# A tiled FFT-domain convolution: frequency ranges of the first tiles, the last tile's scratch in parts, and inverse work behind the last round

## The chip, the cores and the metric

The kernel runs on one core of a Trainium2 chip. The metric is the device time of one execution in microseconds (us). Eight runs of the kernel before gave a median of 279.88 us (278.17 to 282.5). All other numbers come from one further execution that the hardware profiler recorded.

The core has five engines that run their own instruction streams and wait for each other by semaphores: TensorE (PE in the profile; PEld is its weight load), VectorE (DVE), ScalarE (ACT), GpSimd (POOL) and SyncE (SP), which here only issues DMAs. TensorE writes its products into eight PSUM banks; VectorE and ScalarE copy ("evacuate") them to SBUF.

## The reference

```
x: (1, 224, 224, 96) bf16    w: (7, 7, 96, 96) bf16
wp = pad(w, H and W up to 224)
Yf = einsum('bhwi,hwio->bhwo', rfft2(x), rfft2(wp))
y  = irfft2(Yf, (224, 224)).astype(bf16)
```

This is a circular convolution of a 224 x 224 image of 96 channels with a 7 x 7 kernel, 96 channels in and 96 out.

## The kernel before

The kernel transforms only along the height, by small DFT matrices, and convolves along the width directly. The height is cut into 8 blocks of B = 28 rows; each needs L = 34 input rows, which give NS = 17 frequencies with a real and an imaginary part. The width is cut into NT = 7 tiles of 32 columns, numbered 0 to 6 in the code; the text counts them first to seventh, and the seventh (TL = 6) is the last one. Even and odd columns are kept apart as two phases.

Each tile passes three stages:

- *Forward.* TensorE multiplies the pixels of one column (118 rows, four of the eight blocks at a time) with the DFT matrix `Fm`; the result goes through PSUM into `xf`, by channel, frequency, column and block. For the tiles from the fourth on, `a_jobs` makes all 17 frequencies of a column with one matmul of 136 columns. For the first three tiles `f_jobs(t, part)` does it by frequency ranges, so that the rounds of the first frequencies can begin early; the limits are in `SH2`. A tile's `xf` begins with three columns (the halo) that `new_xf` copies on ScalarE from the tile before, one copy per phase and range. The buffers `xf` alternate between tiles.
- *Rounds.* `b_round(t, s, ...)` handles one frequency s: 33 matmuls of 96 columns, with the input planes as stationary operand (from `xf` and from `J`, sums and differences of planes that `jit` makes on VectorE, three frequencies as one group) and the transformed filters `WF` as moving operand. ScalarE copies a part of the products to `tt_`, VectorE makes `u` and `v`, and the sum of `v` and `u` goes to `yf` on GpSimd or, in some rounds (`ydve`), on VectorE. After a group of frequencies (`YGRP`) the `yf` tile is written to a scratch tensor in DRAM (`scr`).
- *Inverse.* The scratch is read back with frequency and block in the partitions (`tt`), and `c_jobs(t)` makes 11 jobs of two matmuls each with the inverse DFT matrix `G`; each job's two products are copied out and written to the result. Loads for these jobs are issued by `queue_c` in round 3 of the next tile (all are issued by SP) as far as buffers are free.

The rounds of the first two tiles are interleaved with lag `LAG` = 4; r counts these steps. From the third tile on, tiles follow one another. Everything else (filter transform in the first two tiles, forward of the next tile, inverse jobs of the two tiles before) is put between the matmuls of the rounds as filler. A queue entry `add(a, b, jobs)` spreads its jobs evenly over the slots a to b; a round s has slots 2s (`mid`) and 2s + 1 (`end`). How many inverse jobs run in each tile is in `CQ`: (jobs left from two tiles before, jobs of the tile before). In the loop over tiles, `km` is the slot where the old ones end and the new ones begin, and `k1` the slot where all must be done.

Which engine evacuates a PSUM bank is decided by `evac` when the program is built, from running estimates `load["v"]` and `load["a"]`.

The last tile has no rounds after it to hide its inverse. Its scratch has separate tensors: `scra` for frequencies 0 to 8 and `scrb` 0 and 1 for 9 to 14 and 15 to 16. `scra` is loaded in round 11. At the end `load_b` loads the other two; the inverse is then done with all blocks at once: `first` multiplies with `GA` (frequencies 0 to 8), `WARM` matmuls on zeros keep TensorE running, and `second` adds the product with `GB`. The copies alternate between VectorE and ScalarE (`tail_evac`). `GA` and `GB` are put together from `G` by 20 small DMAs (`g_parts`), one per round in the fourth and fifth tiles.

The writes of the last tile's `yf` are put in a list `puts` and issued from ScalarE's queue in the round after, but for the last one, which SP issues.

Of the kernel before, what the change touches and what calls it, by code (L numbers as in the profile page):

```python
# [8 lines left out]
BF16 = mybir.dt.bfloat16  # L9
# [5 lines left out]
B = 28  # L15
# [28 lines left out]
WARM = 36  # L44
BIAS = 3000.0


# [5 lines left out]
def kernel(  # L53
# [76 lines left out]
    def dma(out_ap, in_ap):  # L130
        return DE.dma_start(out=out_ap, in_=in_ap)
# [9 lines left out]
    KB = (NJ * 2 * (SB - SA), NJ * 2 * (NS - SB))  # L141
    assert sum(KB) == 128
    XW = 2 * TW * C
    xn_bufs = [cpool.tile([R, XW + 32], BF16, name=f"xn{i}") for i in range(2)]

# [320 lines left out]
    def b_round(t, s, mid, end, ydve=False, planes=()):  # L466
# [26 lines left out]
        if s == 0:  # L493
            for part in range(2):
                conv(b0, part * C, 0, part)
            SE.copy(out=tt_[:, 0:2 * C], in_=b0[:, 0:2 * C])
            mid()
            for mi, m in enumerate((2, 1)):
                for part in range(2):
                    conv(b1, (mi * 2 + part) * C, m, part)  # L500
            VE.tensor_tensor(out=yv.rearrange("p r m o -> p m r o"),
                             in0=tt_[:, 0:2 * C].rearrange("p (r o) -> p r o", o=C).unsqueeze(1).to_broadcast([128, 2, 2, C]),
                             in1=b1[:, 0:4 * C].rearrange("p (m r o) -> p m r o", m=2, r=2), op=ALU.add)
            load["a"] += 110 + 0.9 * 192
            load["v"] += 540
            for f in planes:
                f()
            end()
        else:
            v = tv_pool.tile([128, 2, 2, C], F32, name="v")  # L510
            if merge:
                conv(b0, 2 * C, 0, 0, both=True)
                conv(b0, 2 * C, 2, 0, add=True)
                conv(b0, 3 * C, 1, 0, add=True)
                conv(b0, 0, 0, 1)
                conv(b0, C, 0, 2)
# [37 lines left out]
        if s == y1 - 1:  # L554
            dst, yo0 = scr_tiles[t], 0
            if t == TL:
                i = (s >= SA) + (s >= SB)
                dst, yo0 = scr_tiles[(t, i)], (0, SA, SB)[i]

            def put(eng=DE):  # L560
                eng.dma_start(out=dst.rearrange("w j s e -> (w j) s e")[:, y0 - yo0:y1 - yo0],
                              in_=yf[:, 0:y1 - y0].rearrange("p s r m o -> p s (r m o)"))
            if t == TL and s < NS - 1:
                puts.append(lambda: put(SE))
            else:
                put()
# [20 lines left out]
    tl_a = [tl_all[0:KA, g * TW2:(g + 1) * TW2].rearrange("p (w e) -> p w e", e=2 * C) for g in range(2)]  # L587
    tl_b = tl_all[:, 2 * TW2:3 * TW2].rearrange("p (w e) -> p w e", e=2 * C)

    def load_b(i, eng, nh):  # L590
        sb = scr_tiles[(TL, 1 + i)].rearrange("w j s (r e) -> (j s r) w e", r=2)
        for h in range(nh):
            w0, w1 = h * TW // nh, (h + 1) * TW // nh
            eng.dma_start(out=tl_b[i * KB[0]:i * KB[0] + KB[i], w0:w1], in_=sb[:, w0:w1])

    def g_parts():
        for j in range(4):
            dma(GA[j * 2 * SA:(j + 1) * 2 * SA, j * B:(j + 1) * B], G[0:2 * SA, 0:B])
            yield
        for j in range(NJ):  # L600
            for i, (s, s1) in enumerate(((SA, SB), (SB, NS))):
                n = 2 * (s1 - s)
                dma(GB[i * KB[0] + j * n:i * KB[0] + (j + 1) * n, j // 4, j % 4 * B:(j % 4 + 1) * B], G[2 * s:2 * s1, 0:B])
                yield

    yo_free = [J_bufs[2][0:4 * B, i * PXC * C:(i + 1) * PXC * C] for i in range(2)]
# [63 lines left out]
    for jg in range(2):  # L670
        for f in a_bank(0, xf0, xh_bufs[jg], 0, 3, jg, 0):
            f()
    fj = [f_jobs(0, p) for p in range(3)]
    for p in range(3):
        for f in fj[p][0]:
            f()
    for _ in range(3):
# [48 lines left out]
    nburst = len(bursts)  # L726
    for r in range(NS + LAG):
        if r == 0:
            add(0, 4, fj[1][1] + fj[2][1])
        for p in range(3):  # L730
            if r == (1, 3, 5)[p]:
                new_xf(1, SH2[p], SH2[p + 1])
                fj = f_jobs(1, p)
                if p == 2:
# [3 lines left out]
        for p in range(3):  # L738
            if r == SH2[p + 1] + 1 - (p == 2):
                new_xf(2, SH2[p], SH2[p + 1])  # L740
                fj = f_jobs(2, p)
                if p == 2:
# [32 lines left out]
    for t in range(2, NT):  # L775
        if t == TL:
            scr_tiles[t] = None
            scr_tiles[(t, 0)] = dr_pool.tile([TW, NJ, SA, 4 * C], BF16, name="scra")
            for i in range(2):
                scr_tiles[(t, 1 + i)] = dr_pool.tile([TW, NJ, (SB - SA, NS - SB)[i], 4 * C], BF16, name=f"scrb{i}")  # L780
# [17 lines left out]
        for s in range(NS):  # L798
# [3 lines left out]
                now = jit(t, g + 1) if g + 1 < len(JGB) else jit(t + 1, 0)  # L802
            if s == 3:
                queue_c(t - 1)
            if t in (3, 4):
                next(gp, None)
            if t == TL and s == SA + 2:
                sv = scr_tiles[(TL, 0)].rearrange("w j s (r e) -> (j s r) w e", r=2)
                for g in range(2):
                    for p0, p1 in ((0, 64), (64, KA)):  # L810
                        dma(tl_a[g][p0:p1], sv[g * KA + p0:g * KA + p1])
            b_round(t, s, fills(qs, 2 * s), fills(qs, 2 * s + 1), bool(now) or (t == TL and s >= NS - 3), now)
    tail[0] = 2
    assert not cj and not pend
# [22 lines left out]
    for i, (g, q) in enumerate(order):  # L837
# [41 lines left out]
```

## Time and profile before

| | us |
|---|---|
| median of 8 runs | 279.88 |
| the profiled execution | 280.32 |
| its span in the trace | 278.6 |
| first round begins | 22.3 |
| fourth to sixth tiles and most of the third | about 100 to 227 |
| last tile's rounds begin on TensorE | 227.1 |
| last sum `yf` ends | 261.0 |
| first product with `GB` | 268.56 |
| last copy ends | 272.9 |

The page shows for each engine the busy time and its share of the span. Its second part cuts the span into 40 slices of 7 us and gives each engine's busy share in tenths; PEclk is the clock that TensorE was granted, in tenths.

```profile
PE   8979998999999999999999999999999997999791
```

The costliest groups, with the mean ns of one instruction, are these; the matmul's duration includes its latency, so that starts lie closer together than durations:

```profile
L85 PE MATMUL pb<-WF,J 96*128 96x96 bf16 x2898 | 168.3, 206 | 0.8 <-DVE WF L85 0.3
...
L85 POOL TENSOR_TENSOR yf<-v,u 128x384 bf16<-128x384 f32 x85 | 84.6, 1011 | 150.1 <-issue 96.4
...
L85 ACT CAST xf<-pb 96x408 bf16<-96x408 f32 (+2 forms) x147 | 68.8, 486 | 6.4 <-PE pb L85 4.3
...
L85 DVE TENSOR_TENSOR J<-xf 96x1824 bf16<-96x1824 bf16 (+1 forms) x84 | 60.0, 753 | 0.1
...
L85 PE MATMUL pb<-Fm,xn 118*128 118x136 bf16 (+3 forms) x640 | 45.7, 199 | 0.4 <-DVE u L85 0.4
...
L85 PE MATMUL pb<-tt,Gm 102*84 102x384 bf16 (+1 forms) x132 | 33.0, 331 | 2.3 <-DMA tt<-scr 2.3
```

All are on line 85, because a helper issues every instruction; the names of the tiles tell what they are. The last column is the engine's idle time just before such an instruction, and what ended most of it.

### The profile page before, as it was taken

Reading aid. Unit: us, or ns where it says so; the run is one execution under the profiler, and the core shown is the slowest. Engines: PE = TensorE matmul, PEld = TensorE weight load, DVE = VectorE, ACT = ScalarE, POOL = GpSimd, SP = SyncE. Lnnn points to the kernel's source line nnn. Section 1 sums busy time; section 2 is a strip of 40 time slices with the busy share of each in tenths; the row PEclk is TensorE's granted clock in tenths of the full one; section 3 lists DMA queues with packets and bytes.
Section 4 is the critical chain, followed back from the end, with each engine's and each line's share of the span. In section 5 each row is a group of like instructions: output and inputs, shape, how many; then the busy total and the mean of one; then the engine's idle time right before and its main releaser. Section 6 shows DMA issues by size and latency. Waiting matters only on the chain. (4 is left out here: it accounts for less than half of the span.)

```text
span 278.6 us, 12291 instructions
## 1 busy us (share of the span) xinstructions
PE 263.8 (95%) x5226; PEld 242.3 (87%) x5226; DVE 218.8 (79%) x457; ACT 198.9 (71%) x489; POOL 98.0 (35%) x146
## 2 busy tenths in 40 slices
PE   8979998999999999999999999999999997999791
PEld 3659898999999999999999999999999996889670
DVE  5538899898799798779887888779788899488432
ACT  5539996677964767988988799887989855475122
POOL 7720032443545745323422423341532242223000
PEclk9999999999999999999999999999999999799997
DMA  7957010722111497798975496989498428755955
GB/s 185 214 108 200 16 47 2 232 68 87 45 47 46 146 260 133 228 282 225 285 204 180 115 292 166 274 192 336 155 208 249 144 94 212 194 157 166 236 121 164
DMA packets 46038, 46.79 MB, mean 168 GB/s; under 512 B 35150, under 2 KB 36954, under 8 KB 45886
## 3 DMA queue, kind: packets, MB, share of 16 engines
q1 hardware_dynamic: 43696, 43.94, 57.7%
q10 hardware_dynamic: 2288, 2.06, 2.6%
q8 instruction: 41, 0.67, 1.1%
q14 instruction: 13, 0.11, 0.1%
HBM read 24.65 MB, written 21.33 MB: 165 GB/s over the span
## 5 line engine op out<-in xcount | busy, mean ns | idle before, releaser
L85 PE MATMUL pb<-WF,J 96*128 96x96 bf16 x2898 | 168.3, 206 | 0.8 <-DVE WF L85 0.3
L85 PEld LDWEIGHTS <-J 96*128 96x128 bf16 x2898 | 142.8, 98 | 10.7 <-issue 1.6
L85 POOL TENSOR_TENSOR yf<-v,u 128x384 bf16<-128x384 f32 x85 | 84.6, 1011 | 150.1 <-issue 96.4
L85 ACT CAST xf<-pb 96x408 bf16<-96x408 f32 (+2 forms) x147 | 68.8, 486 | 6.4 <-PE pb L85 4.3
L85 PE MATMUL pb<-WF,xf 96*128 96x96 bf16 x952 | 60.6, 207 | 1.2 <-DVE WF L85 0.6
L85 DVE TENSOR_TENSOR J<-xf 96x1824 bf16<-96x1824 bf16 (+1 forms) x84 | 60.0, 753 | 0.1
L85 PEld LDWEIGHTS <-xf 96*128 96x128 bf16 x952 | 47.4, 98 | 1.6 <-issue 1.0
L85 PE MATMUL pb<-Fm,xn 118*128 118x136 bf16 (+3 forms) x640 | 45.7, 199 | 0.4 <-DVE u L85 0.4
L85 PE MATMUL pb<-tt,Gm 102*84 102x384 bf16 (+1 forms) x132 | 33.0, 331 | 2.3 <-DMA tt<-scr 2.3
L85 ACT CAST WF<-pb 96x480 bf16<-96x480 f32 (+1 forms) x58 | 28.6, 572 | 7.3 <-PE pb L85 7.3
L85 ACT CAST J<-pb 84x384 bf16<-84x384 f32 (+1 forms) x66 | 28.3, 483 | 6.1 <-PE pb L85 3.1
L85 ACT CAST yo<-pb 84x384 bf16<-84x384 f32 (+1 forms) x66 | 28.1, 483 | 4.7 <-PE pb L85 4.7
L85 PEld LDWEIGHTS <-xn 118*128 118x128 bf16 x640 | 30.5, 97 | 0.5 <-issue 0.5
L85 DVE TENSOR_TENSOR J<-J 96x912 bf16<-96x912 bf16 (+1 forms) x42 | 25.0, 595 | 0.0
L85 PE MATMUL pb<-wq 98*128 98x120 bf16 (+1 forms) x288 | 21.3, 226 | 1.4 <-DMA wq<-in_w_dram 1.4
L85 PEld LDWEIGHTS <-wq 98*128 98x128 bf16 x288 | 19.4, 150 | 1.9 <-issue 1.9
L85 PE MATMUL pb<-wu 128*128 128x512 bf16 (+1 forms) x80 | 17.8, 385 | 1.0 <-DVE ct L85 1.0
L85 PEld LDWEIGHTS <-wu 128*128 128x128 bf16 (+1 forms) x80 | 9.3, 118 | 8.5 <-issue 2.7
L85 DVE TENSOR_TENSOR yf<-v,u 128x384 bf16<-128x384 f32 x27 | 15.5, 574 | 0.9
L85 DVE CAST WF<-pb 96x480 bf16<-96x480 f32 (+1 forms) x14 | 8.1, 612 | 7.6 <-PE pb L85 7.5
L85 PEld LDWEIGHTS <-Gm 102*84 102x84 bf16 (+1 forms) x132 | 11.1, 118 | 3.0 <-DMA tt<-scr 2.4
L85 ACT COPY xf<-xf 96x816 bf16<-96x816 bf16 (+3 forms) x20 | 11.1, 616 | 0.0
(391 smaller groups left out, 228.8 us busy)
## 6 DMA issues: line engine op xcount, KB each, us to landing
scr<-yf SPq DMA_DIRECT2D x30, 288.0 KB
xn<-in_x_dram SPq DMA_DIRECT2D x12, 672.0 KB
tt<-scr SPq DMA_DIRECT2D x24, 336.0 KB
out_dram<-yo SPq DMA_DIRECT2D x12, 252.0 KB
out_dram<-J SPq DMA_DIRECT2D x12, 252.0 KB
tt<-scr SPq DMA_DIRECT2D x6, 288.0 KB
wq<-in_w_dram SPq DMA_DIRECT2D x1, 1719.0 KB
WF<-in_x_dram SPq DMA_DIRECT2D x2, 672.0 KB
```

The costliest lines, as they stand in the source:

```text
L85: r = fn(*a, **k)
```

## The change

- `SH2` has two ranges, 0 to 7 and 8 to 16, instead of three; `f_jobs` of the first three tiles is called for two parts. The second range has 72 columns per matmul (9 frequencies, two parts, four blocks). In the second tile the ranges start in steps r = 1 and 3 (before 1, 3, 5), in the third in r = 9 and 17 (before 9, 14, 17).
- The last tile's scratch has six tensors of three frequencies (the last of two), `PARTS`. `load_p(i)` loads one of them: parts 0 to 3 in rounds 6, 9, 12 and 15, parts 4 and 5 after the last round, all issued by SP. The order of rows in `GA` and `GB` follows, so `g_parts` issues 36 DMAs, now in the fourth to sixth tiles.
- The last part's write is issued by ScalarE.
- `CQ`: of the inverse jobs, the fifth tile's rounds run 13 instead of 14, the sixth tile's 12 instead of 14, the last tile's 10 instead of 14. The seven that are left, all of the sixth tile, stand behind the last round, before `first`. In the last tile the old jobs fill slots 3 to 15 and the new ones follow until slot 26.
- `WARM` is 20 instead of 36.
- The result of the last tile is written in eight DMAs of 8 columns instead of four of 16.
- One estimate for VectorE's load in the first two tiles is 350 instead of 250.

```diff
-SB = 15
+PARTS = (0, 3, 6, 9, 12, 15, 17)
...
-CQ = {2: (11, 0), 3: (11, 2), 4: (9, 5), 5: (6, 8), 6: (3, 11)}
-SH2 = (0, 8, 13, 17)
+CQ = {2: (11, 0), 3: (11, 2), 4: (9, 4), 5: (7, 5), 6: (6, 4)}
+SH2 = (0, 8, 17)
...
-WARM = 36
+WARM = 20
...
+    prt = []
+    for a, b in zip(PARTS[:-1], PARTS[1:]):
+        prt.append((a, b, int(a >= SA), (4 if a < SA else NJ) * 2 * (a - (0 if a < SA else SA))))
...
-            load["v"] += (560 if ydve else 250 if t < 2 else 0) + (560 if merge else 900)
+            load["v"] += (560 if ydve else 350 if t < 2 else 0) + (560 if merge else 900)
...
-                i = (s >= SA) + (s >= SB)
-                dst, yo0 = scr_tiles[(t, i)], (0, SA, SB)[i]
+                i = sum(s >= b for b in PARTS[1:])
+                dst, yo0 = scr_tiles[(t, i)], PARTS[i]
...
-            if t == TL and s < NS - 1:
+            if t == TL and s == NS - 1:
+                put(SE)
+            elif t == TL:
                 puts.append(lambda: put(SE))
...
-    def load_b(i, eng, nh):
...
+    def load_p(i):
+        a, b, h, r0 = prt[i]
+        sv = scr_tiles[(TL, i)].rearrange("w j s (r e) -> (j s r) w e", r=2)
+        n = 2 * (b - a)
+        if h:
+            dma(tl_b[r0:r0 + NJ * n], sv)
+        else:
+            for g in range(2):
+                dma(tl_a[g][r0:r0 + 4 * n], sv[g * 4 * n:(g + 1) * 4 * n])
...
     def g_parts():
...
+        for a, b, h, r0 in prt:
+            n = 2 * (b - a)
+            for j in range(NJ if h else 4):
...
-            if r == (1, 3, 5)[p]:
+            if r == (1, 3)[p]:
...
-                add(2 * r + 1, 2 * r + (5, 5, 4)[p], fj[0] + fj[1])
+                add(2 * r + 1, 2 * r + (5, 8)[p], fj[0] + fj[1])
...
-            if r == SH2[p + 1] + 1 - (p == 2):
+            if r == (9, 17)[p]:
...
-                add(2 * r, 2 * r + (8, 7, 5)[p], fj[0] + fj[1])
+                add(2 * r, 2 * r + (10, 6)[p], fj[0] + fj[1])
...
-        k1 = 2 * NS if t < TL else 2 * NS - 6
+        k1 = 2 * NS if t < TL else 2 * NS - 8
...
+        if t == TL:
+            km = 15
...
-            if t in (3, 4):
+            if t in (3, 4, 5):
                 next(gp, None)
-            if t == TL and s == SA + 2:
...
+            if t == TL:
+                for i, (_, b, _, _) in enumerate(prt[:4]):
+                    if s == b + 3:
+                        load_p(i)
...
-    load_b(0, SE, 2)
-    load_b(1, DE, 1)
+    load_p(4)
+    load_p(5)
+    for f in cj:
+        f()
...
-        if q % 4 == 3:
-            w0 = TL * 2 * TW + q // 4 * PXC
-            dma(out[0, g * M4:(g + 1) * M4, w0:w0 + PXC, :].rearrange("h w c -> h (w c)"), yo[0:M4])
+        if q % 2:
+            w0, o0 = TL * 2 * TW + (q - 1) * 4, (q - 1) % 4 * 4 * C
+            dma(out[0, g * M4:(g + 1) * M4, w0:w0 + 8, :].rearrange("h w c -> h (w c)"), yo[0:M4, o0:o0 + 8 * C])
```

More of the change, by code (lines that the diff above doesn't have):

```diff
@@ L140 @@
     KA = 4 * 2 * SA
-    KB = (NJ * 2 * (SB - SA), NJ * 2 * (NS - SB))
-    assert sum(KB) == 128
+    prt = []
+    for a, b in zip(PARTS[:-1], PARTS[1:]):
+        prt.append((a, b, int(a >= SA), (4 if a < SA else NJ) * 2 * (a - (0 if a < SA else SA))))
+    assert SA in PARTS and NJ * 2 * (NS - SA) == 128
     XW = 2 * TW * C
@@ L588 @@
     tl_b = tl_all[:, 2 * TW2:3 * TW2].rearrange("p (w e) -> p w e", e=2 * C)
-    def load_b(i, eng, nh):
[L591 to L594, printed above, removed]
-    def g_parts():
[L597 to L603, printed above, removed]
+    def load_p(i):
[7 more added lines that the diff above has]
+                dma(tl_a[g][r0:r0 + 4 * n], sv[g * 4 * n:(g + 1) * 4 * n])
+    def g_parts():
+        for a, b, h, r0 in prt:
+            n = 2 * (b - a)
+            for j in range(NJ if h else 4):
+                o = GB[r0 + j * n:r0 + (j + 1) * n, j // 4] if h else GA[r0 + j * n:r0 + (j + 1) * n]
+                dma(o[:, j % 4 * B:(j % 4 + 1) * B], G[2 * a:2 * b, 0:B])
                 yield
@@ L672 @@
             f()
-    fj = [f_jobs(0, p) for p in range(3)]
-    for p in range(3):
+    fj = [f_jobs(0, p) for p in range(2)]
+    for p in range(2):
         for f in fj[p][0]:
@@ L728 @@
         if r == 0:
-            add(0, 4, fj[1][1] + fj[2][1])
-        for p in range(3):
-            if r == (1, 3, 5)[p]:
+            add(0, 4, fj[1][1])
+        for p in range(2):
+            if r == (1, 3)[p]:
                 new_xf(1, SH2[p], SH2[p + 1])
                 fj = f_jobs(1, p)
-                if p == 2:
+                if p == 1:
                     for jg in range(2):
                         fj[jg][-1] = then_load(fj[jg][-1], 2, jg)
-                add(2 * r + 1, 2 * r + (5, 5, 4)[p], fj[0] + fj[1])
-        for p in range(3):
-            if r == SH2[p + 1] + 1 - (p == 2):
+                add(2 * r + 1, 2 * r + (5, 8)[p], fj[0] + fj[1])
+        for p in range(2):
+            if r == (9, 17)[p]:
                 new_xf(2, SH2[p], SH2[p + 1])
                 fj = f_jobs(2, p)
-                if p == 2:
+                if p == 1:
                     for jg in range(2):
                         fj[jg][-1] = then_load(fj[jg][-1], 3, jg)
-                add(2 * r, 2 * r + (8, 7, 5)[p], fj[0] + fj[1])
+                add(2 * r, 2 * r + (10, 6)[p], fj[0] + fj[1])
         if r == PGRP[-2][1] + 1:
@@ L777 @@
             scr_tiles[t] = None
-            scr_tiles[(t, 0)] = dr_pool.tile([TW, NJ, SA, 4 * C], BF16, name="scra")
-            for i in range(2):
-                scr_tiles[(t, 1 + i)] = dr_pool.tile([TW, NJ, (SB - SA, NS - SB)[i], 4 * C], BF16, name=f"scrb{i}")
+            for i, (a, b, _, _) in enumerate(prt):
+                scr_tiles[(t, i)] = dr_pool.tile([TW, NJ, b - a, 4 * C], BF16, name=f"scrl{i}")
         else:
@@ L804 @@
                 queue_c(t - 1)
-            if t in (3, 4):
+            if t in (3, 4, 5):
                 next(gp, None)
-            if t == TL and s == SA + 2:
[L808 to L811, printed above, removed]
+            if t == TL:
+                for i, (_, b, _, _) in enumerate(prt[:4]):
+                    if s == b + 3:
+                        load_p(i)
             b_round(t, s, fills(qs, 2 * s), fills(qs, 2 * s + 1), bool(now) or (t == TL and s >= NS - 3), now)
     tail[0] = 2
-    assert not cj and not pend
-    load_b(0, SE, 2)
-    load_b(1, DE, 1)
+    assert not pend
+    load_p(4)
+    load_p(5)
+    for f in cj:
+        f()
     if NP2:
```

## The prediction

> **What bounds the kernel now.** I read the page first, then busy time by stretches, then the order of time where a stretch looked wrong, then the chain.
>
> ```profile
> PE 263.8 (95%) x5226; PEld 242.3 (87%) x5226; DVE 218.8 (79%) x457; ACT 198.9 (71%) x489; POOL 98.0 (35%) x146
> ...
> PEclk9999999999999999999999999999999999799997
> ```
>
> TensorE is the bound almost everywhere, at full clock but for slice 35 (index 34) and the last. The stretches:
>
> ```profile
> core 0: us, PE busy (x) PEld busy (x) DVE busy (x) ACT busy (x) POOL busy (x), PEclk, DMA share, GB/s
> ...
> 36.00:50.00 14.00, 13.27 (x334) 13.08 (x333) 13.74 (x26) 11.16 (x30) 4.37 (x5) 1.00 0.11 41
> ...
> 99.80:228.10 128.30, 127.90 (x2563) 119.84 (x2560) 107.74 (x227) 107.81 (x276) 44.48 (x45) 1.00 0.77 214
> 228.17:234.75 6.58, 6.58 (x139) 6.15 (x136) 6.11 (x13) 2.94 (x8) 3.48 (x4) 1.00 0.51 136
> 234.75:241.00 6.25, 3.99 (x45) 3.44 (x44) 3.04 (x8) 3.17 (x8) 0.99 (x1) 0.73 0.85 190
> ...
> 228.17:261.00 32.83, 29.77 (x561) 27.07 (x558) 26.76 (x56) 17.31 (x44) 10.37 (x11) 0.95 0.70 176
> ```
>
> From 99.8 to 228.1 TensorE has no gap. From 36 to 50 VectorE is as full (13.74 of 14) and TensorE idles 0.73. From 234.75 to 241 something is wrong: 3.99 busy of 6.25 at clock 0.73. In order of time:
>
> ```profile
> 231.67 7.50 SPq L85 DMA_DIRECT2D tt<-scr  x7
> ...
> 237.06 0.72 PE L85 MATMUL pb<-tt,Gm 102*84 102x384 bf16 x2 [2.26 <-DMA tt<-scr]
> ...
> 237.90 0.84 PE L85 MATMUL pb<-WF,xf 96*128 96x96 bf16 x8
> ```
>
> The first inverse job of the sixth tile waits for its load, and afterwards TensorE runs slow: eight matmuls take 0.84 where they otherwise show 0.50. The end:
>
> ```profile
> 261.03 0.35 SPq L85 DMA_DIRECT2D scrb<-yf  x1
> ...
> 262.35 5.82 PEld L85 LDWEIGHTS <-wu 128*112 128x112 bf16 x36
> ...
> 264.31 0.33 SPq L85 DMA_DIRECT2D xf<-scrb  x1
> ...
> 268.56 0.97 PE L85 MATMUL pb<-xf,GB 128*112 128x384 bf16 x5
> ...
> 270.01 3.77 SPq L85 DMA_DIRECT2D out_dram<-tt  x4
> ```
>
> The last sum ends at 261.0; its round trip through DRAM and the 36 filler matmuls both last until about 268.5, so 7.56 us hold no useful TensorE work except four first products. Then come 4.4 us of copies and a write that lands 3.3 us after its issue (the waits of SP's queue).
>
> **What the Trainium skill says.** "TensorE: Matmul & The Clock Gate", Back-to-back issue gap: small matmuls have a floor of about 25 ns, wider ones take N/2.4 + 2.5 ns. The trace agrees: 24 of 40 columns run from 91.77 to the next start at 92.37 (25 ns each), 16 of 32 columns in 0.41 (26), 8 of 64 in 0.23 (29), 6 of 136 in 0.36 (60). Same page, What's actually happening: an idle TensorE falls to half clock by windows of 3.4 us, which run free. Here 2.26 us idle dropped it, and 1.64 us idle (260.2 to 261.84) did not. "DMA: Bandwidth & Descriptors", Two DMAs through the same engine are not ordered: a reader must wait for the writer's semaphore; here the load of the last part issues 3.3 us after its write does. Same page, Issuing engines are not separate DMA queues: so putting the last write on ScalarE's queue buys no bandwidth, as far as this trace can say.
>
> **The change, part by part.** Gains are in us of the profiled execution (280.32, span 278.6, so 1.7 around it; the median, 279.88, is 0.44 lower).
>
> 1. *Forward in two ranges.* Per tile, 64 positions (two halves of rows, 16 columns, two phases) had three matmuls, 29 + 26 + 26 = 81 ns, and now have two: 29 and one of 72 columns, which the trace lacks; the bounds are 29 (the 64-column row) and 60 (136 columns), the page's formula gives 32.5, an estimate that I take. The saving is 19 ns x 64 = 1.2 per tile (at 60 ns it would be a loss of 0.5). Half of the first tile's lies before the weights arrive at 17.8 and is hidden. Left are 2.5 x 1.2 = 3.1 of TensorE time. Evacuations stay 20 per tile with the same elements; two halo copies go in each of the second and third tile (ScalarE, about 0.3 each). The new estimate of 350 for VectorE moves little: in the instruction order, copies of the weights and the forward on VectorE go from 19 to 19. So VectorE keeps its 13.74 of 36 to 50, where most of the second tile's last two ranges sit: I credit 0.3 of its 1.2. Of the first tile's 0.6, with ScalarE at 12.78 of 13.7 there, 0.3. For the third tile the second range is now one block in rounds 17 to 20, with 12 copies on ScalarE instead of 4: 12 x 0.45 + 4 x 0.31 + 1.2 of halo = 7.8 against TensorE's 4 x 1.40 + 64 x 0.0325 = 7.7, balanced; the rounds 14 to 16 before it lose their filler and then run at 1.40 each on TensorE, against about 1.48 on VectorE (u and v together 0.81, a J group of 2.0 per three rounds). I credit 0.7 of 1.2. Sum 1.3; from 0 (VectorE sets it all) to 3.1.
>
> 2. *Jobs moved out of the fifth and sixth tiles' rounds.* The job counts per tile go from 14 and 14 to 13 and 12. A job's two matmuls hold TensorE 0.33 (229.44 to 229.77). 3 x 0.33 = 1.0 in the stretch without a gap; ScalarE, at 84%, loses work too. Full credit: 1.0.
>
> 3. *The last tile's rounds.* Before, tile 5's first job is due at slot 9, 3 us after its load could issue (231.67, when the scratch had landed). Now six old jobs fill slots 3 to 15 and the first new one comes at slot 15, three rounds (over 4.2 us) later, while the data took until 237.06, 2.26 beyond slot 9. The stall of 2.26 goes, and so does the slow clock after it: 237.06 to 240.94 took 3.88 where the same sequence takes 2.24 at full clock, so 1.64. Four fewer jobs: 1.3. TensorE alone: 5.2. What is late next is VectorE: it has 26.76 busy in 32.83, and 32.83 - 5.2 = 27.6 would ask 97% of it. It reached 98% in 36 to 50, but with TensorE idling 5%. I take 28.6, a gain of 4.2; between 3.3 (29.5, VectorE at 91%) and 5.2.
>
> 4. *Six parts.* Same bytes. Loads of parts 0 to 3 are issued in rounds 6, 9, 12 and 15, three rounds after their writes (about 4.8 us; a write of 288 KB took 4.83 with its issue in the chain). They may hold SP up to 1 us each; behind them stand the loads for jobs that now run at the end, and outputs with four buffers. Cost 0; uncovered, at most 1. The 36 small copies into GA and GB instead of 20 go on SP between, in three tiles instead of two: 0.
>
> 5. *The end.* Call T0 the end of the last sum. The last write is on ScalarE's queue; behind it wait ScalarE's job copies, 0.33 later than T0. The 14 job copies at 0.55 and 0.48 alternate: done at T0 + 3.9. The banks keep eight job matmuls before T0, the rest and the eight first products follow the copies; then 20 fillers x 0.163 = 3.3. The second products start at T0 + 7.3, against 7.56. The last part's load issues at T0 + 3.3 as before, but besides it only 288 KB load instead of 576, so it lands by then: 6.3 to 7.5. The job outputs (six) issue on SP behind that load. After that 4.4 of copies as before; outputs leave in eight parts, and the last is 168 KB instead of 336: I take 0.4 off the 3.3; from 0 to 0.8. Sum 0.2 + 0.4 = 0.6; from -1.5 (half clock for the fillers' first half) to 1.5.
>
> Sum: 1.3 + 1.0 + 4.2 + 0 + 0.6 = 7.1: 273.2 for the profiled execution, 272.8 for the median.
>
> **Rivals.** *VectorE sets the loops:* part 1 gives 0, part 3 gives 3.3, the end 0.6: 4.9, so 275.0. For it: 13.74 of 14. Against: in 78 to 93 TensorE was solid without filler in several rounds. *TensorE alone sets them:* 3.1 + 1.0 + 5.2 + 1.0 = 10.3, so 269.6. *The stall comes back* at slot 15, because the load is later than before (SP held by part 0): with 2.3 to 3.9 lost, 276. Against: three rounds of slack, and the load issues before part 0's. *A cold end (slower):* between the last round and T0 + 3.9 TensorE has 2.3 of work in 5.4 us; if the clock halves there and stays down, 20 fillers cost 3.3 more, 8 first products 1.3, and the 24 matmuls of the finish 7.8 instead of 4.4: the finish then ends at T0 + 19.7 instead of 12.0, and with 0.4 off the last write that is 7.3 lost against the 6.5 of parts 1 to 3: 280.7, or 282.9 if VectorE sets the loops too. It decides from the point where the slow clock lasts through the finish; for it: slice 35; against: 1.64 us idle did no harm, and the gaps here are shorter.
>
> **How the numbers follow.** Forecast 0.57, VectorE 0.19, TensorE alone 0.08, stall 0.06, cold end 0.10. The forecast's own range is 271 to 274.5; the VectorE case takes it to 276, TensorE alone to 269.6: 269.5 to 276.5. Anything within 0.5% (278.5 to 281.3) cannot be told from no change. Faster 0.90; of the cold end's 0.10 half ends within the bound and half, with VectorE's loops, above it: same 0.05, slower 0.05.
>
> **What would show it.** No wait on tt<-scr near the last tile and clock 1.00 there; the last tile's 32.83 down to about 28.6 with VectorE over 90%; 128 forward matmuls per tile in the first three, with little TensorE idle from 36 to 50 more than 0.73; second products 7.3 after the last sum. It is wrong if VectorE's waits open TensorE gaps of over 1 us in the last tile, or if the clock falls in the end.

## The result, and the profile after

| | before | after |
|---|---|---|
| median of the timed runs, us | 281.12 (55 runs) | 283.63 (20 runs) |
| ratio to before, 95% interval | | 1.0104 [1.0081, 1.0126] |
| profiled execution / span, us | 280.32 / 278.6 | 282.29 / 280.6 |

The change makes the kernel 1.0% slower; forecast was a gain of 2.5%. The ratio is taken from the faster of the two states in which executions of one kernel are found, so it isn't the quotient of the medians. Two parts of the page of after, busy time and slices:

```profile
PE 260.3 (93%) x5018; PEld 237.6 (85%) x5018; DVE 221.5 (79%) x464; ACT 195.9 (70%) x478; POOL 98.1 (35%) x146
...
PE   8889898999999999999999999999999999898393
...
PEclk9999999999999999999999999999999999999579
```

TensorE has 3.5 us less to do than before (260.3 against 263.8), and the weak slice near the last tile is gone. But in the third slice from the end it is now busy three tenths, and its clock there is five tenths. The stretches: 36 to 50 as before (a fixed time, so not quite the same work), then the last tile's rounds (227.50 to 257.33), the time from the last sum to the first product with `GB` (257.33 to 271.54), and two parts of that:

```profile
core 0: us, PE busy (x) PEld busy (x) DVE busy (x) ACT busy (x) POOL busy (x), PEclk, DMA share, GB/s
36.00:50.00 14.00, 12.39 (x272) 12.02 (x269) 12.91 (x24) 10.79 (x28) 4.19 (x5) 1.00 0.28 83
...
227.50:257.33 29.83, 28.12 (x553) 25.16 (x551) 26.60 (x57) 14.21 (x37) 11.62 (x11) 1.00 0.61 164
257.33:271.54 14.21, 9.07 (x34) 5.83 (x34) 3.42 (x7) 2.93 (x7) 0.00 (x0) 0.64 0.85 195
260.00:264.00 4.00, 0.03 (x1) 0.06 (x2) 1.12 (x3) 0.85 (x2) 0.00 (x0) 0.50 0.81 175
264.00:270.00 6.00, 6.00 (x19) 4.00 (x20) 0.00 (x0) 0.00 (x0) 0.00 (x0) 0.50 1.13 234
```

The last tile's rounds are shorter by 3.3 (30.01 against 33.29 in the table below) and at full clock; forecast was 4.2. The stretch after them, which took 7.56, takes 14.21 at a mean clock of 0.64. TensorE in order of time there:

```profile
263.97 2.78 PE L85 MATMUL pb<-xf,GA 72*112 72x384 bf16 x8 [4.43 <-DMA xf<-scrl]
266.54 5.16 PE L85 MATMUL pb<-wu 128*112 128x384 bf16 x20
271.54 0.98 PE L85 MATMUL pb<-xf,GB 128*112 128x384 bf16 x5
```

The first products wait 4.43 us, from 259.54 on, for a load from scratch. The eight products and most of the 20 fillers then run at half clock, but the clock did not fall after the wait: from 260.00 on it is already at a half. SP's queue shows why the load is late (start, duration of the group, what is issued):

```profile
232.59 4.61 SPq L85 DMA_DIRECT2D tt<-scr  x6
243.37 0.34 SPq L85 DMA_DIRECT2D out_dram<-yo  x1
...
245.89 0.38 SPq L85 DMA_DIRECT2D out_dram<-J  x1
253.11 0.31 SPq L85 DMA_DIRECT2D tt<-scr  x1
...
259.77 0.34 SPq L85 DMA_DIRECT2D out_dram<-yo  x1
260.19 3.32 SPq L85 DMA_DIRECT2D xf<-scrl  x5
```

Between 237.2 and 243.4, 246.3 and 253.1, 255.1 and 259.8 the queue issues nothing. Five loads for parts 2 to 5, 1056 KB, go out together after the last write, although parts 2 and 3 were written much earlier. What SP waited for between 227 and 272, before and after (total, times, longest):

```profile
SPq L85 <- DMA scra<-yf: 7.7, 2, 6.1
```

```profile
SPq L85 <- DMA scrl<-yf: 17.5, 3, 6.8
```

In after, SP waits for writes that ScalarE issued. The built program says which. There, the DMAs of SP and of ScalarE share eight completion semaphores, dealt out in turn, in an order that the build assumes. In this program a DMA is not issued before the earlier holder of its semaphore has completed, whichever engine issued that one. For the changed kernel:

| issued by SP | also waits for ScalarE's write of |
|---|---|
| an output of a sixth-tile job (243.37) | part 1 (issued 240.28) |
| a load for a sixth-tile job (253.11) | part 3 (250.69) |
| an output of a sixth-tile job (259.77) | part 4 (254.76) |
| the first load of part 2 (260.19) | part 5, the last (257.36) |

None of the four needs the data of the write it waits for, but an engine issues in order, so all that stands behind them waits too. The first three rows are the three waits of the 17.5; the fourth adds none in this trace, because part 5's write has landed by the time its turn comes. In before two job outputs share a semaphore with writes of `scra` in this way, and one of them is the wait of 6.1; the rest of the 7.7 is the load of `scra` waiting for its own data. No load that TensorE needed at once stood behind that output.

### The profile page after: what moved, and what is told of

The parts are those of the page before. It is cut to its first block, busy times and chain, and to the rows that moved or that the text cites. A ratio compares the mean times of both kernels' runs of the same rounds, so it can differ in the third digit from the quotient of the medians.

```text
span 280.6 us, 11905 instructions
## 1 busy us (share of the span) xinstructions
PE 260.3 (93%) x5018; PEld 237.6 (85%) x5018; DVE 221.5 (79%) x464; ACT 195.9 (70%) x478; POOL 98.1 (35%) x146
## 4 chain that ended last, share of the span: by engine, by line
PE 57%; DVE 15%; DMA 10%; ACT 7%; issue 6%; POOL 3%; SPq 1%; ACTq 0%; DVEq 0%; POOLq 0%
PE pb L85 57%; DVE J L85 6%; DMA wq<-in_w_dram 5%; DMA scrl<-yf 3%; ACT WF L85 3%; DVE v L85 3%; POOL yf L85 3%; DVE WF L85 2%; ACT xf L85 2%; DVE u L85 2%; DVE yf L85 2%; DMA xf<-scrl 1%; SPq L85 1%; DMA tt<-scr 0%; DVE xf L85 0%
## 5 line engine op out<-in xcount | busy, mean ns | idle before, releaser
L85 PE MATMUL pb<-WF,J 96*128 96x96 bf16 x2898 | 166.2, 206 | 4.5 <-DVE u L85 2.4
L85 ACT CAST xf<-pb 96x408 bf16<-96x408 f32 (+4 forms) x146 | 68.0, 492 | 7.4 <-PE pb L85 3.9
L85 PE MATMUL pb<-Fm,xn 118*128 118x136 bf16 (+2 forms) x512 | 43.0, 208 | 0.3 <-DVE u L85 0.2
L85 ACT CAST yo<-pb 84x384 bf16<-84x384 f32 (+1 forms) x62 | 26.5, 480 | 9.5 <-PE pb L85 4.4
L85 ACT CAST J<-pb 84x384 bf16<-84x384 f32 (+1 forms) x63 | 27.1, 485 | 4.8 <-PE pb L85 4.7
L85 PEld LDWEIGHTS <-xn 118*128 118x128 bf16 x512 | 27.8, 98 | 0.6 <-issue 0.5
L85 PE MATMUL pb<-wu 128*128 128x512 bf16 (+1 forms) x64 | 16.4, 423 | 1.1 <-DVE ct L85 1.1
L85 PEld LDWEIGHTS <-wu 128*128 128x128 bf16 (+1 forms) x64 | 8.1, 130 | 8.4 <-issue 1.9
L85 DVE TENSOR_TENSOR WF<-WF 96x960 bf16<-96x960 bf16 x15 | 10.9, 776 | 0.0
```

The source lines that it names most:

```text
L85: r = fn(*a, **k)
```

## The experiments

*Theory Q*: SP's queue stands still because its DMAs draw semaphores of ScalarE's writes; the late load, the idle TensorE and its slow clock follow. *Rival J*: the jobs behind the last round and their copies make the end long. All ratios are to the kernel before, with 95% intervals. Sections come from one trace each: from ScalarE's first `tt_` copy of a tile to that of the next; T0 is the end of the last sum, GB the first product with `GB`.

| run | ratio | first three tiles | 5th + 6th | last, to T0 | T0 to GB | rest |
|---|---|---|---|---|---|---|
| before | 1 | 109.11 | 63.61 | 33.29 | 7.56 | 10.04 |
| after | 1.0104 | 110.19 | 62.69 | 30.01 | 14.21 | 9.06 |
| e1_puts_sp | 0.9872 | 110.21 | 62.67 | 29.31 | 6.72 | 8.84 |
| e2_jobs_in | 0.9965 | 110.18 | 63.60 | 29.95 | 8.62 | 8.97 |
| e3_fwd3 | 1.0052 | 109.58 | 62.68 | 28.69 | 15.93 | 9.77 |
| e4_fwd2_only | 0.9951 | 110.73 | 63.61 | 30.60 | 9.01 | 9.91 |
| e5_before_again | 1.0039 | 109.19 | 63.61 | 34.56 | 7.71 | 9.96 |
| e6_before_puts_sp | 1.0086 | 109.14 | 63.61 | 35.94 | 7.31 | 9.99 |
| e7_parts3 | 1.0016 | 110.27 | 62.67 | 29.60 | 12.27 | 9.02 |
| e8_fwd3_puts_sp | 0.9822 | 109.24 | 62.67 | 28.82 | 8.37 | 10.25 |
| e9_last_sp | 1.0056 | 110.64 | 62.68 | 29.97 | 13.28 | 8.89 |
| e10_last_act | 1.0129 | 110.29 | 62.68 | 28.83 | 15.06 | 8.81 |
| e11_jobs_in_puts_sp | 1.0062 | 110.39 | 63.61 | 36.28 | 5.69 | 8.83 |
| e12_warm0 | 1.0102 | 111.09 | 62.68 | 29.63 | 11.11 | 10.50 |

The fourth tile takes 32.13 or 32.14 in all. One warning comes first: e5 is the kernel before itself and shows 1.0039 [1.0006, 1.0072]. Ratios that differ by 0.4% are therefore not told apart, and a difference of 0.5% is little more than that.

**e1: all writes of the last tile on SP, in the program's order**

```diff
-            if t == TL and s == NS - 1:
-                put(SE)
-            elif t == TL:
-                puts.append(lambda: put(SE))
-            else:
-                put()
+            put()
```

> The changed kernel, but all six scratch writes of the last tile are issued by SP in program order instead of by ScalarE. Theory Q (SP stands still in the last tile because its DMAs share eight completion semaphores with ScalarE's writes, so that loads of parts 1 to 5 come only after the last write): with no DMA on ScalarE's queue the loads of parts 0 to 3 issue in their rounds, the idle of 4.4 us before the first products goes, the clock stays up, and the second products start about 7.5 us after the last sum instead of 14.2: some 6 us less than the changed kernel, ratio to before about 0.98 to 0.99. Rival J (the seven inverse jobs behind the last round hold the end up by themselves): no more than 1 us less than the changed kernel, ratio about 1.01.

Measured: 0.9872 [0.9811, 0.9934] (6 executions), 2.3% below the changed kernel, with the same jobs behind the last round. TensorE at the end:

```profile
260.50 1.97 PE L85 MATMUL pb<-xf,GA 72*112 72x384 bf16 x8
262.31 3.41 PE L85 MATMUL pb<-wu 128*112 128x384 bf16 x20
265.56 0.98 PE L85 MATMUL pb<-xf,GB 128*112 128x384 bf16 x5
```

From T0 (258.84 here, 257.33 in after) to the second products it is 6.72 instead of 14.21. Of these 7.49, 4.98 is the first products' start (T0 + 1.66 against T0 + 6.64), 0.76 the first products at full instead of half clock (262.31 - 260.50 against 266.54 - 263.97), 1.75 the fillers likewise. SP's wait on these writes falls from 17.5 to 4.3.

Q holds for the queue: the loads go out in time, and the 4.98 is the idle time that goes. J falls as the cause of the stall, since the seven jobs stand behind the last round here too; what they cost by themselves e11 shows. Whether the 2.51 of slow clock also came from the late load is another question, which e8 takes up.

**e2: the job counts, the due times and the 36 fillers of before; parts and forward as changed**

```diff
+CQ = {2: (11, 0), 3: (11, 2), 4: (9, 5), 5: (6, 8), 6: (3, 11)}
+WARM = 36
+        k1 = 2 * NS if t < TL else 2 * NS - 6
-        if t == TL:
-            km = 15
```

> The changed kernel with all inverse jobs back in the rounds (the counts, due slots and 36 fillers of before), six parts and two ranges kept. Theory J: the end is as before, so the loss in it goes, about 5.7 us less than the changed kernel, less the 3 to 4 us that the last tile's rounds gain: ratio 1.00 to 1.005. Theory Q: SP still waits for ScalarE's writes, but by the program's semaphores part 2 no longer waits for the last write, only part 3 for part 4's: the first products come earlier than in the changed kernel, but part 3's load (288 KB) still joins parts 4 and 5 at the end; second products about 8 to 10 us after the last sum; ratio 1.005 to 1.02, since the wait for the sixth tile's load comes back too.

Measured: 0.9965 [0.9934, 0.9997]. With other DMAs between them the semaphores fall differently: SP waits 11.1 on the writes, no wait over 4.5, the loads of part 2 go out at 253.03, and T0 to GB is 8.62, in Q's range of 8 to 10. The ratio is below both theories' ranges: the wait for the sixth tile's load, which Q had coming back, is only 0.54 here, and the last tile takes 29.95. So removing the moved jobs also repairs most of the end. Taken alone this run would have spoken for J; e1, which keeps the jobs there, shows that it is the order in the queue.

**e3: the changed kernel with the forward in three ranges**

```diff
-SH2 = (0, 8, 17)
+SH2 = (0, 8, 13, 17)
```

(with the calls, steps and due times of before)

> The changed kernel with the forward of the first three tiles in three ranges again. Theory F (two ranges cost about 1 us: VectorE sets the rounds 9 to 17 and the third tile's copies are bunched at its start; fourth tile's first copy 1.1 us later after the first round than before): 1 us less than the changed kernel, ratio about 1.007. Rival (the prediction's sum: fewer matmuls save 1.3): 1.3 us more, ratio about 1.015.

Measured: 1.0052 [1.0023, 1.008], 0.5% below after, nearer to F than to its rival; the first three tiles take 0.6 less, the end stalls as in after (15.93).

**e4: the kernel before with the forward in two ranges alone**

> The kernel before with the forward of the first three tiles in two ranges and nothing else. Theory F: 1 us more than before, ratio 1.004. The prediction's sum: 1.3 us less, ratio 0.995. The last tile is as before, its stall of 2.3 us and slow clock too.

Measured: 0.9951 [0.9921, 0.9982]. By the ratio the prediction's sum is met and F is not; by the trace its first three tiles take 1.6 longer than before's. The last tile makes it up (30.60 against 33.29), at full clock, and nothing in the edit touches the last tile. That is not this one execution alone: the median of the mean clock over all 22 executions of e4 is 0.992, over the 59 of before in the same series 0.986. Why the last tile keeps its clock more often here is open; e5 bears on it.

**e5: the kernel before once more**

> The kernel before, once more, for a second trace. Theory V (the 2.26 us wait for tt<-scr in the last tile, and the 1.64 us of slow clock behind it, are in some executions only): a trace with a mean clock of 0.99 or more has no such wait, its last tile takes about 30.6 us instead of 33.3 and its span is 277 to 277.5; one with a clock near 0.986 has the wait and takes 33 again. Rival W (the wait is in every execution of this kernel): the wait is there whatever the clock. The time against before: ratio 1.00.

Measured: 1.0039 [1.0006, 1.0072]; the trace has a clock of 0.978, so it is theory V's second branch. The first inverse job of the sixth tile in the last tile, in e5 and in e4:

```profile
237.70 0.87 PE L85 MATMUL pb<-tt,Gm 102*84 102x384 bf16 x2 [1.94 <-DMA tt<-scr]
...
238.68 0.84 PE L85 MATMUL pb<-WF,xf 96*128 96x96 bf16 x8
```

```profile
236.55 0.52 PE L85 MATMUL pb<-tt,Gm 102*84 102x384 bf16 x2 [1.19 <-DMA tt<-scr]
```

The wait is in both; after 1.94 eight matmuls take 0.84, after 1.19 they take 0.50. So this run does not decide between V and W: both traces of this kernel have the wait and the slow clock, and no trace was taken of an execution with a high clock. There are such executions: the four fastest of e5's 20 (279.01 to 279.55) have a clock of 0.993 or more. In the three traces here the job always waits, by an amount that varies, and the slow clock comes with the longer waits. How much of e4's gain is a shorter wait and how much is the 0.4% of uncertainty stays open; two ranges do not shorten the first three tiles in any trace.

**e6: the kernel before with the last tile's writes on SP**

```diff
-            if t == TL and s < NS - 1:
-                puts.append(lambda: put(SE))
-            else:
-                put()
+            put()
```

> The kernel before, with the last tile's writes to scratch issued by SP in the program's order instead of by ScalarE. Theory Q (a DMA of SP can stand behind a ScalarE write that shares its completion semaphore, and the whole queue with it): in before one output waited 7.7 us for a write of part 0, with the first loads for the last part behind it, but nothing that TensorE needed at once; so SP's waits on scra<-yf go, and the time changes by -0.3 to +0.5%. If the 2.26 us wait for tt<-scr came from the same cause, the last tile is about 2 to 4 us shorter: ratio 0.985 to 0.993. Rival J (the jobs behind the last round make after slow): nothing to gain here, ratio 0.998 to 1.005, and the waits of SP's queue in the trace carry no weight.

Measured: 1.0086 [1.0053, 1.0119], slower, which neither theory had (0.5% even against e5). SP in order:

```profile
235.20 0.32 SPq L85 DMA_DIRECT2D scra<-yf  x1
235.69 6.66 SPq L85 DMA_DIRECT2D tt<-scr  x7
```

The write of the first three frequencies stands ahead of the job loads and waits for its `yf`, so these issue at 235.69 instead of 231.67, and the job due at slot 9 waits 4.07. In e1, where the first such job is due at slot 15 and fewer jobs run in the last tile, it waits 0.78. So the repair of e1 seems to need the later slot that the change brought; no run moves the slot alone.

**e7: the changed kernel with three parts**

```diff
-PARTS = (0, 3, 6, 9, 12, 15, 17)
+PARTS = (0, 9, 15, 17)
```

(part 0 is loaded in round 12, the others after the last round)

> The changed kernel with the last tile's scratch in three parts (groups 0 to 8, 9 to 14, 15 and 16, as before) and all else of the change. Theory Q with the six parts as what exposes it: no load sits between the writes except the one of part 0, so fewer DMAs of SP draw the semaphore of a late write; by the built program one output still waits for the write of groups 9 to 11, and none of the last loads waits for a write that isn't its own. The last part's load issues about 3.3 us after the last write as before, first products start about T0 + 6.5 to 7.5, ratio 0.985 to 0.995. Rival K (six waiting jobs at the end and 20 fillers make after slow whatever the parts): T0 + 11 or more stays, ratio 1.005 to 1.012.

Measured: 1.0016 [0.9988, 1.0044]: below after, but above Q's range, and T0 to GB is 12.27, as rival K had it. K's ratio isn't met either.

```profile
254.86 0.34 SPq L85 DMA_DIRECT2D out_dram<-yo  x1
255.29 9.62 SPq L85 DMA_DIRECT2D xf<-scrl  x4
```

The one output that Q had counted (it waits for a write of part 1) was enough: it holds the queue from 248.3 (the end of the issues before it) to 254.9, and the loads of all three parts follow it. SP waits 20.7 on the writes here: 6.6 and 6.5 ahead of this output and an earlier one, the rest ahead of loads that need the data. So six parts are not needed for the stall; I had priced the number of such waits, not what stands behind each.

**e8: three ranges and all writes on SP**

> The changed kernel with both repairs: last tile's writes issued by SP in program order, and the forward in three ranges. If the two gains found alone (1.28% from the issuing engine, and about 0.5% from three ranges against two within the changed kernel) add up: 1.0104 - 0.0232 - 0.0052 = 0.982, about 276.2 us. Theory F (the two ranges cost TensorE 1.1 to 2 us through VectorE's waits in the second tile, nothing gives it back): ratio 0.980 to 0.985 and the stretch from the first to the fourth tile about 109.6. Rival G (the forward's time is made up by a shorter wait in the last tile): ratio as with SP's writes alone, 0.985 to 0.990.

Measured: 0.9822 [0.9768, 0.9875], 276.0 us median of 6 runs. This is the best kernel of the study and beats both; the first three tiles take 109.24, near F's 109.6, and the ratio is what adding the two gains gave. Its interval overlaps e1's, so that three ranges beat two by 0.5% is supported by e3 and the traces, not by this pair alone. Its end is 1.65 longer than e1's, because the clock falls there, though its queue doesn't stand (stretches of e8, columns as above):

```profile
255.00:257.00 2.00, 1.45 (x7) 0.64 (x6) 2.00 (x5) 1.03 (x3) 0.00 (x0) 1.00 0.84 222
...
259.00:261.00 2.00, 2.00 (x8) 1.30 (x7) 0.00 (x0) 0.00 (x0) 0.00 (x0) 0.50 0.53 138
```

TensorE is fully busy while the clock is at 0.50; the pauses lie up to 4 us earlier and are no longer than e1's in the same place (0.18 and 0.41), where the clock stayed at 1.00. What decides between the two is open.

So the clock can fall at the end without a late load. It did in the changed kernels too. The last six job matmuls, before the wait for the load, and the first products after it, in e3 (first two lines) and the same six in after:

```profile
256.72 2.36 PE L85 MATMUL pb<-tt,Gm 102*84 102x384 bf16 x6 [0.73 <-DVE yo L85]
264.09 2.78 PE L85 MATMUL pb<-xf,GA 72*112 72x384 bf16 x8 [5.01 <-DMA xf<-scrl]
```

```profile
257.84 1.70 PE L85 MATMUL pb<-tt,Gm 102*84 102x384 bf16 x6 [0.73 <-DVE yo L85]
```

In e3 the six take 2.36 instead of 1.70: the clock halves under them at about 257.5, 1.6 before the wait of 5.01 begins. In the 15 us before that, TensorE's longest pause is 0.73. In after the clock halves 0.3 into the wait. Of the eight traces with jobs behind the last round, seven show such a fall between 257 and 262, all but e1's; of the six with the jobs inside the rounds, only e2's does. And e1's own executions differ: the four fastest, with its trace among them, have a mean clock of 0.987 to 0.991, the other two 0.980 and 0.975 (278.81 and 279.49 us).

**e9 and e10: which write is on ScalarE** (e9: only the last is on SP; e10: only the last is on ScalarE)

```diff
 e9
-            if t == TL and s == NS - 1:
-                put(SE)
-            elif t == TL:
+            if t == TL and s < NS - 1:
                 puts.append(lambda: put(SE))
 e10
             if t == TL and s == NS - 1:
                 put(SE)
-            elif t == TL:
-                puts.append(lambda: put(SE))
             else:
                 put()
```

> The changed kernel with one edit: the write of the last part (groups 15 and 16) is issued by SP, as in before; the other five of the last tile stay on ScalarE. In the built program no DMA of SP then waits for the last write but its own load; an output still waits for the write of part 1, another for that of part 3, and the loads of part 2 for that of part 4. Theory Q: SP's queue still stands (2 to 8 us) for parts 1 and 3, but its loads of parts 2 to 4 no longer stand behind the last write; the first products start about 258 to 261 and not 263.97, T0 to second products 7 to 9.5 us instead of 14.2, ratio 0.985 to 0.995. Rival L (it is the number of writes on ScalarE, not which one): little change, T0 + 12 or more, ratio above 1.003.

> The mirror of the run before: of the last tile's six writes only the last is issued by ScalarE, the other five by SP in program order. In the built program the output of one job (a yo) then waits for this last write, and behind it in SP's queue stand the writes of parts 3 and 4 and the loads of parts 2 to 5. Theory Q: this is worse than the changed kernel, though five of six writes are where the best run had them: the write of part 3 can't issue before the last write has landed (T0 + 2.8), a second round trip follows, T0 to second products 14 to 18 us, ratio 1.01 to 1.03. Rival L (the number of writes on ScalarE counts): near the run with all writes on SP, ratio 0.985 to 0.995.

Measured: e9 1.0056 [1.0029, 1.0083], where Q's 0.985 to 0.995 fails and rival L's numbers are met. e10 1.0129 [1.0074, 1.0184], T0 to GB 15.06, where Q is met and L fails. SP in e9, then in e10:

```profile
259.73 1.23 SPq L85 DMA_DIRECT2D xf<-scrl  x3
261.06 0.47 SPq L85 DMA_DIRECT2D scrl<-yf  x1
261.57 4.87 SPq L85 DMA_DIRECT2D xf<-scrl  x2
```

```profile
258.34 0.34 SPq L85 DMA_DIRECT2D out_dram<-yo  x1
258.77 0.34 SPq L85 DMA_DIRECT2D scrl<-yf  x1
259.21 1.28 SPq L85 DMA_DIRECT2D xf<-scrl  x2
260.60 0.49 SPq L85 DMA_DIRECT2D scrl<-yf  x1
262.10 3.65 SPq L85 DMA_DIRECT2D xf<-scrl  x3
```

In e9 two long waits (6.4 each) go before, for the writes of parts 1 and 3; the loads of part 2 wait for ScalarE's write of part 4, and the last write, ready at T0 = 257.83, stands behind them until 261.06. In e10 one single write on ScalarE is enough: a job's output draws its semaphore, waits for it until 258.34 (the longest wait is 9.0), and the writes of parts 3 and 4, whose data the earlier rounds had made, queue behind the output. With five of the six writes taken from ScalarE and none of e1's gain, neither the time that the issues take ScalarE (0.33 each) nor the earlier place of the writes explains e1. What decides is not the number of such writes or the place of one, but whether anything on SP draws a semaphore of one that comes late.

**e11: e1 with the jobs, due times and fillers of before**

> The changed kernel with all last-tile writes on SP, but with the job counts, the due times and the 36 filler matmuls of before (no jobs behind the last round). It prices the moved jobs where nothing stalls the end. My prediction's part 2 and part 3 (1.0 for three jobs out of tiles 5 and 6; the wait for tt<-scr at slot 9 comes back): the fifth and sixth tiles are 0.9 longer together, the last tile's first new job waits 2 us or more for its load, since SP now issues the write of part 0 ahead of these loads, and the slow clock follows: last tile 33 to 36 us against 29.3, ratio 1.000 to 1.010. Rival M (the moved jobs are worth only their own TensorE time): 0.990 to 0.995.

Measured: 1.0062 [1.0033, 1.0091]; the fifth and sixth tiles are 0.94 longer than in e1, the last tile 6.97, just above the range given.

Its first new job waits 3.92 for its load. With a clean queue the moved jobs and their later due slots are together worth 1.9% (1.0062 against 0.9872, from two series); rival M's 0.990 to 0.995 is out. Its end, 5.69, is the shortest of all, 1.03 less than e1's with 16 fillers more: the jobs behind the last round seem to have a price there, though a smaller one than the 6.97 of the last tile.

**e12: the changed kernel without fillers**

```diff
-WARM = 20
+WARM = 0
```

> The changed kernel without the 20 filler matmuls ahead of the second products (the output is the same). They took 5.16 us of its end at half clock, from 266.54. Theory Q2 (the last load had landed by about 268, so the fillers, not the data, hold the second products from then on): second products start 3 to 4 us earlier, but without a warm-up all 24 run at half clock: about 7.8 us instead of 4.4, which gives back most of it; time -1 to +1 us against the changed kernel, ratio 1.005 to 1.015. Rival R (the data came late, about 271): second products start within 0.7 us of where they were and the finish is slower, ratio 1.015 to 1.025.

Measured: 1.0102 [1.007, 1.0133], no difference from after. TensorE at the end:

```profile
264.18 2.78 PE L85 MATMUL pb<-xf,GA 72*112 72x384 bf16 x8 [3.63 <-DMA xf<-scrl]
269.10 1.82 PE L85 MATMUL pb<-xf,GB 128*112 128x384 bf16 x5 [2.14 <-DMA xf<-scrl]
```

The second products now wait for their data, and start 3.1 nearer to T0 than in after (11.11 against 14.21), where the fillers still held them. The rest of the span takes 1.44 more, since the products begin at half clock. Q2 holds: the fillers at half clock are part of the 14.21, but without them the time is the same.

## Why the prediction was wrong

By its steps, against the sections of the traces; together the sections give the 2.0 by which the span grew (-0.55 before the first round, +1.08, 0, -0.92, -3.28, +6.65, -0.98). From the forecast of -7.1 that is 9.1 away: 6.9 of it in the end up to the second products, 2.4 in the forward, 0.9 in the last tile's rounds, and 1.1 back in the rest.

1. *Forward, forecast -1.3.* Wrong sign: +1.08 over the first three tiles (+0.63, +1.49, -1.04), where the lower bound of the step was 0. What a matmul saves was estimated rightly: 72 columns start 32 ns apart in after. TensorE's busy time in the three tiles falls by 2.0 (107.37 to 105.36), but its idle time grows by 3.1 (1.74 to 4.83). From 36 to 50 it idles 1.61 where it idled 0.73, against the sign that the prediction had named. What TensorE waited for from 23 to 105 in after (total, times, longest; in before the three come to 0.9, 0.2 and 0.4):

```profile
PE pb L85 <- DVE WF L85: 2.0, 3, 1.0
PE pb L85 <- DVE J L85: 1.3, 3, 0.5
PE pb L85 <- DVE u L85: 1.2, 3, 0.5
```

   Waits on VectorE go from 1.5 to 4.5. The rival "VectorE sets the loops" named this engine but stopped at 0, and VectorE is not full there: it is busy 40.65 of the first tile's 45.53 and 28.09 of the second's 33.62. So VectorE's sum of work does not set these stretches either; the waits come with the new order of the work, and which part of it makes them (longer pieces of filler, later starts) is not shown. Three ranges in its place gain 0.6 (after to e3) and 1.0 (e1 to e8) in the traces; the times are less clear (e4).
2. *Jobs out of the fifth and sixth tiles, -1.0.* Right: -0.92, and back by 0.94 in e11.
3. *Last tile's rounds, -4.2.* The mechanism was right; the size, 3.28, is VectorE's figure, which the step had as its lower end: no wait on `tt<-scr` is left, the clock is 1.00, VectorE has 26.60 in 29.83. The size depends on the execution before: its wait of 2.26 and the slow clock behind it are not equally long in each (e5: 1.94).
4. *Six parts, "Cost 0; uncovered, at most 1".* This is the step that failed. It priced SP's load instructions at a microsecond each and looked for who is behind them, but it took for granted that a DMA waits only for its own data and buffers. Instead DMAs of SP waited for ScalarE's writes, whose semaphores they share: SP stood still three times, 17.5 us in all, and the first products started 4.98 later than in e1, where only the issuing of the writes differs. It is this assumption that fails, not the number of parts (e7).
5. *The end, -0.6.* It follows from step 4: "the last part's load issues at T0 + 3.3 as before, but besides it only 288 KB load" became a first load of part 2 at T0 + 2.86 with 1056 KB in five loads. +6.65 up to the second products, of which 2.51 (against e1) is slow clock; the step had that only as the end of its range, with 1.5. The rest was better than forecast, -0.98 against -0.4. Where the queue didn't stand (e1), the step was right within 0.6: 6.72 against the forecast 7.3.

With 7.49 of the stall taken out, e1's span is 274.4, against a forecast of about 271.5 for the span (278.6 - 7.1): the difference is in the forward (2.4) and in a first round that began 1.7 later than in the profile of before, less 1.4 by which the end and the finish were better.

The rival of a cold end, at 280.7 or 282.9, came near the measured time, and half of its mechanism is in the traces. It had the clock fall through gaps of ordinary copies, and the clock did fall there: in e3 and e12 before the wait for the load, in after 0.3 into it, in e8 with no late load at all. The argument against it, "1.64 us idle did no harm, and the gaps here are shorter", did not hold. The prediction had named a fall of the clock at the end as a sign of being wrong, and it came. What the rival had wrong is that the clock stays down through the finish: in after it is full again for the second products. So of the 7.49 between after and e1, 4.98 is shown to be the queue's; for the 2.51 of slow clock that is not shown. In e8, with a clean queue, such a fall cost 1.65.

"DMA: Bandwidth & Descriptors" (Issuing engines are not separate DMA queues) says that starting DMAs from more engines only saves the sequencer's issue time. I had read it as "no harm". The runs show a cost that the sentence leaves out: six writes moved off ScalarE took 2.3% off the changed kernel.

## What to carry to other kernels

Before a transfer is moved to another engine's queue, or a load is put between others, list what each DMA in that queue waits for in the built program, shared completion semaphores included, and what stands behind it; a wait that is harmless today is the first place to look. Read the waits of the queues in the profile of before even where they cost nothing: 6.1 us of SP waiting for a transfer it didn't need was there to be seen. And less work for the busiest engine is a gain only if the new order of the work opens no waits: here 2.0 us less of it came with 3.1 us more of idle time.

## What the runs showed that I had not expected

- One write on another queue held SP for 9.0 us (e10), with two finished parts' writes behind it.
- TensorE's clock: in the last tile half clock came with idle times of 1.94, 2.26, 3.92 and 4.07 us, and not with 0.54, 0.78 and 1.19; nor did it come with 1.64 at the end of before and 1.89 at the end of e4. The length of the pause alone does not decide. "TensorE: Matmul & The Clock Gate" (What's actually happening) speaks of one idle window of about 3.4 us; here 1.94 sufficed, and in e8 pauses of 0.18 and 0.41, with the slow clock 2.8 us after the second.
- The same repair, writes on SP, is worth -2.3% in one kernel and about +0.5 to +0.9% in the other (e5, e6), where one job, due earlier, has its load behind the first write.
- The same program differed from itself by 0.4% between series of runs, with an interval that leaves out 1.
